# Paired output stores, a second queue for the last tiles, other quads, and a list scheduler with measured lengths

**Chip, cores, metric.** One core of one Trainium2 chip. The metric is the device time of one execution in microseconds (us); lower is better.

**Terms.** In this kernel TensorE does the matrix products, VectorE, ScalarE and GpSimd the element-wise work, and SyncE issues transfers. The profile calls them PE, DVE, ACT, POOL and SP; PEld is TensorE's weight loads, and a q (SPq, ACTq) marks the queue from which an engine issues transfers. SBUF is the on-chip memory in which the kernel's buffers lie. A transfer *lands* when its completion is signalled.

## The reference

A small speech model, two convolutions with stride 2, a projection, and a joint network. What matters here is the end: for every batch entry, time step and label step a tanh of a sum, times a 512 x 512 matrix, 16,000 rows of output.

```python
h = gelu(conv5(x, w1))[:, ::2, :]            # B=2, T=4000, D=512
f = gelu(conv5(h, w2))[:, ::2, :]            # 1000 rows for each batch entry
fe = f @ w_f                                  # (2, 1000, 512)
ge = g @ w_g                                  # (2, 8, 512)
j = tanh(fe[:, :, None, :] + ge[:, None, :, :])
return j @ w_o                                # (2, 1000, 8, 512), bfloat16
```

## The kernel before

The program is not written in the order in which it runs. Each operation is put into a plan with the buffers it reads and writes and an assumed length; a list scheduler simulates the engines with these lengths, orders each engine's queue, repeats this for 16 rounds with adjusted urgencies, and keeps the round that ends first. So an assumed length costs nothing by itself, but decides the order.

```python
def simulate(self, pred, succ, late):
    ...
        i = min(now) if e in ("pe", "sp") else min(now, key=lambda i: (late[i], i))
        ...
        start[i] = t
        free[e] = t + o.cost          # the assumed length; 0.05 us for a store on SyncE
```

The output is 125 tiles of 128 rows x 512 columns. 57 are plain: four matmuls of 512 columns, a copy to SBUF by VectorE or ScalarE, one store of 128 KB. The other 68 are made in 17 *quads* of four tiles by a seven-product scheme (28 matmuls of 256 columns) that needs sums of the inputs, made by VectorE or, for the 11 late quads, by GpSimd, and several adds on VectorE afterwards. Which quads these are is the list `WQ`; `LEAD` and `TRAIL` say how many plain tiles come before the first late quad and after the last.

```python
WQ = (5,6,10,11,12,13,16,17,18,20,21,22,24,25,26,28,29)
LEAD, TRAIL = 6,2
...
def three():                       # of a quad: tiles 0 and 1 are complete here
    ...
    tt("dve", half(1, 1), v2(y), k15, add)
    tt("dve", half(0, 1), v2(z), u2, add)
    banks.append(z)
    for t in range(2):
        send(c0 + t * P, s1 + s0 + t)          # one store for each tile, on SyncE
...
def joint_tile(jt):                # a plain tile; the last one goes in two halves
    ...
        if h == 1 or (jt % 3 == 2 if early else plain[0] % 3 == 2) and not last:
            act(o, v, ACT.Copy)
        else:
            pl.op("dve", ...tensor_copy..., vec_cost(o, (v,)))
        send(c0, s, cl, ("sp", "act")[h])
```

Of the kernel before, what the change touches and what calls it, by code (L numbers as in the profile page):

```python
# [7 lines left out]
ACT = mybir.ActivationFunctionType  # L8
ALU = mybir.AluOpType
BF16 = mybir.dt.bfloat16  # L10
FP32 = mybir.dt.float32
FP16 = mybir.dt.float16
P = 128
# [297 lines left out]
def bass_standalone__seq2seq_rnn_t_joint__speech_kernel(  # L311
# [21 lines left out]
    U = g.shape[1]  # L333
    NK = D // P
    assert (B, T, D, K, U) == (2, 4000, 512, 5, 8)
    T1, T2 = T // 2, T // 4
# [2 lines left out]
    XW = 528  # L339
    HOFF, HWID = 2, 338  # L340
    RING, LRING = 2048, 4096
    WQ = (5,6,10,11,12,13,16,17,18,20,21,22,24,25,26,28,29)
    LEAD, TRAIL = 6,2
    FROM, LATE = 64 * P, 30
    NSLOT = 12
    BU = B * U
    NT = 512
# [3 lines left out]
    with ExitStack() as es:  # L351
# [56 lines left out]

        def vec_cost(o, ins, fast=True):
            bf = fast and all(not v.psum and v.ap.dtype != FP32 for v in (o,) + tuple(ins))  # L410
            return o.ap.free_size() * (0.52e-3 if bf else 1.04e-3) + 0.065

        def memset(v):
            pl.op("pool", lambda e: e.memset(v.ap, 0.0), (), (v,))  # L414
# [5 lines left out]
        def act(o, i, func, scale=1.0, bias=None, cost=None):  # L420
            rd = (i,) if bias is None else (i, bias)
            pl.op("act", lambda e: e.activation(o.ap, i.ap, func, scale=scale,  # L422
                                                bias=0.0 if bias is None else bias.ap), rd, (o,),
                  cost or o.ap.free_size() * 0.84e-3 + (0.05 if i.psum else 0.17 if i.ap.dtype == FP32 else 0.09))

        def mm(o, pairs, start, stop, check=True):

# [557 lines left out]
        def fe(b):  # L985
            for i, m in ((1, 0), (0, 0), (1, 1), (0, 1), (2, 0), (2, 1), (1, 2), (0, 2), (2, 2), (1, 3), (0, 3), (2, 3)):
                v = ps.cols(bank(), START[i + 1] - START[i])
                sl = slice(START[i], START[i + 1])
                mm(v, [(wf_sb[k, m * P:(m + 1) * P], fT[b][k, sl]) for k in range(NK)], True, True)
                o = feT[b][m, i::3]  # L990
                if i == 1:
                    act(o, v, ACT.Copy, cost=0.54)
                else:
                    pl.op("dve", lambda e, o=o, v=v: e.tensor_copy(out=o.ap, in_=v.ap), (v,), (o,), 0.47)  # L994

        def tanh(v, k, lo=0, hi=T2):

# [44 lines left out]
        def send(c0, slot_, cl=slice(0, 512), eng="sp"):  # L1042

            lo = c0
            while lo < c0 + P:
                vv = lo // T2
                b, u, q = vv // U, vv % U, lo % T2
                n = min((vv + 1) * T2, c0 + P) - lo
                rows = (lo - c0, lo - c0 + n)
                src = oste.rows(*rows, slot_, cl) if slot_ < 4 else (  # L1050
                    ostq.rows(*rows, slot_ - 4, cl) if slot_ < 16 else ostm[slot_ - 16].rows(*rows, cl))
                dst = out[1 - b, q:q + n, u, cl]
                pl.dma(eng, lambda e, src=src, dst=dst: e.dma_start(dst, src.ap), (src,), (), slot_sem[slot_], 2 * n * P * 4)
                lo += n

        def joint_tile(jt):
            c0 = jt * P
            done.add(jt)
            ahead(c0 + P, 900)
            late = c0 >= FROM  # L1060
            r0 = c0 % (LRING if late else RING)
            j = lambda k: jL[k, r0:r0 + P] if late else jT[k][r0:r0 + P]
            early = jt < LATE
            s = jt % 4 + (16 if jt >= 20 else 0) if early else (0, 12, 1, 13, 2, 14, 3, 15)[plain[0] % 8]
            plain[0] += not early
            last = jt == ntile - 1
            for h in range(2 if last else 1):
                w = NT // 2 if last else NT
                cl = slice(h * w, (h + 1) * w)
                v = ps.cols(bank(), w)  # L1070
                mm(v, [(j(k), wo_sb[k, cl]) for k in range(NK)], True, True)
                o = oste[s, cl] if s < 4 else ostq[s - 4, cl] if s < 16 else ostm[s - 16][cl]
                if h == 1 or (jt % 3 == 2 if early else plain[0] % 3 == 2) and not last:
                    act(o, v, ACT.Copy)
                else:
                    pl.op("dve", lambda e, o=o, v=v: e.tensor_copy(out=o.ap, in_=v.ap), (v,), (o,), vec_cost(o, (v,)))  # L1076
                send(c0, s, cl, ("sp", "act")[h])

        def weights_o(wT):
            B_ = [[wo_sb[2 * i:2 * i + 2, 256 * j:256 * j + 256] for j in range(2)] for i in range(2)]  # L1080
# [6 lines left out]
        def quad_steps(q, eng, u=[0]):  # L1087

            c0 = 4 * q * P
            late = c0 >= FROM  # L1090
            soon = jt_w1 > 4 * q
            r0 = c0 % (LRING if late else RING)
            S_, kk = (sAm, kqm) if soon else (sA[u[0] % 3], kq[u[0] % (3 if late else 2)])
            k1, u2, k15 = (kk[i] for i in range(3))
            o_, s1 = (oste, 0) if soon else (ostq, 4)
            s0 = 0 if soon else 4 * (u[0] % 2)
            T_ = wTm if q < 13 else wT
            u[0] += not soon

            def A(i, j, k=None):  # L1100
                lo = r0 + 2 * i * P
                if late:
                    return jL[2 * j:2 * j + 2, lo:lo + 2 * P] if k is None else jL[2 * j + k, lo:lo + 2 * P]
                return jT[2 * j + k][lo:lo + 2 * P]

            v2 = lambda b: ps.cols(b * NT, NT).map(lambda a: a.rearrange("p (t c) -> p t c", t=2))

            def product(a, b, bk, start):
                for t in range(2):
                    sl = slice(t * P, (t + 1) * P)  # L1110
                    mm(ps.cols(bk * NT + 256 * t, 256), [(a(k, sl), b(k)) for k in range(2)], start and t == 0, True, False)

            def Ab(i, j):
                lo = r0 + 2 * i * P
                if late:
                    return lambda k, sl: jL[2 * j + k, lo + sl.start:lo + sl.stop]
                return lambda k, sl: jT[2 * j + k][lo + sl.start:lo + sl.stop]

            Sb = lambda i: lambda k, sl: S_[i, k, sl]
            Bb = lambda i, j: lambda k: wo_sb[2 * i + k, 256 * j:256 * j + 256]  # L1120
            Tb = lambda i: lambda k: T_[i, k]
            half = lambda i, j: o_[s0 + 2 * i:s0 + 2 * i + 2, 256 * j:256 * j + 256]
            held = []

            def sums():
                ahead(c0 + 4 * P, 900 if late else 300)
                for k in (None,) if late else range(2):
                    w = 2 if late else 1
                    cost = (0.58 if eng == "pool" else 0.133) * w + (0 if eng == "pool" else 0.065)
                    S1 = lambda i: S_[i] if late else S_[i, k]  # L1130
                    for o, a, b, op in ((0, A(1, 0, k), A(1, 1, k), add), (2, A(0, 0, k), A(1, 0, k), sub), (1, S1(0), A(0, 0, k), sub),
                                        (3, A(0, 1, k), S1(1), sub)):
                        v = S1(o)
                        pl.op(eng, lambda e, v=v, a=a, b=b, op=op: e.tensor_tensor(out=v.ap, in0=a.ap, in1=b.ap, op=op), (a, b), (v,), cost)  # L1134

            def one():
                held.extend(banks.pop(0) for _ in range(3))
                x, y, z = held
                product(Ab(0, 0), Bb(0, 0), x, True)
                product(Sb(1), Tb(1), y, True)  # L1140
                act(k1, v2(x), ACT.Copy)
                tt("dve", u2, v2(y), k1, add)

            def two():
                x, y, z = held
                product(Sb(0), Tb(0), z, True)
                product(Ab(0, 1), Bb(1, 0), x, False)
                tt("dve", k15, v2(z), k1, add)
                act(half(0, 0), v2(x), ACT.Copy)
                banks.append(x)  # L1150

            def three():
                x, y, z = held
                product(Sb(2), Tb(2), y, False)
                product(Sb(3), Bb(1, 1), z, False)
                tt("dve", half(1, 1), v2(y), k15, add)
                tt("dve", half(0, 1), v2(z), u2, add)
                banks.append(z)
                for t in range(2):
                    send(c0 + t * P, s1 + s0 + t)  # L1160

            def four():
                x, y, z = held
                product(Ab(1, 1), Tb(3), y, False)
                done.update(range(4 * q, 4 * q + 4))
                tt("dve", half(1, 0), v2(y), k1, add)
                banks.append(y)
                for t in range(2, 4):
                    send(c0 + t * P, s1 + s0 + t)

            return [sums, one, two, three, four]

# [130 lines left out]
```

## Time and profile before

| | before |
|---|---|
| device time, median of 3 | 262.35 us (262.25 to 262.76) |
| span of the profiled execution | 261.2 us (its time 262.84, a slow one among its fellows) |
| TensorE busy | 97%, last matmul ends at 256.73 us |
| last copy to SBUF starts (ScalarE) | 256.75 us |
| last store starts (SyncE) | 258.65 us |

The span is what the profile shows, from the first to the last instruction; the time is always longer, by 1.6 us in this kernel. Three stretches: the *front*, up to a group of eight matmuls just behind a stop near 23 us; the *stretch* from that group to the start of the last copy, in which TensorE is the bound; and the *tail*, from the last copy to the end of the span.

### The profile page before, as it was taken

How to read it: one execution, taken by the hardware profiler on the slowest of the kernel's cores; microseconds unless marked ns; L12 is line 12 of the kernel's file. 1: busy time of each engine (PE TensorE's matmuls, PEld its weight loads, DVE VectorE, ACT ScalarE, POOL GpSimd, SP SyncE). 2: the span in 40 equal slices, each digit the busy share in tenths (PEclk: the TensorE clock that was granted, in tenths of full speed). 3: DMA queues.
4: the chain of work that ended last, by engine and by line, in shares of the span. 5: the costliest groups of instructions: out<-in, count | busy, mean ns of one | idle time of the engine just before them, and what ended most of it. 6: DMA issues, size and time to landing. Idle time of an engine off the chain costs nothing.

```text
span 261.2 us, 4927 instructions
## 1 busy us (share of the span) xinstructions
PE 253.3 (97%) x1771; PEld 171.9 (66%) x1786; DVE 227.0 (87%) x447; ACT 189.2 (72%) x316; POOL 56.0 (21%) x64
## 2 busy tenths in 40 slices
PE   8999999999999899999999999999999999999992
PEld 3997764446666556566677744777777677777771
DVE  0999999999999999998557999999957778897883
ACT  2688879984365999667765569748449999999520
POOL 1000004300000000000000000000003999989930
PEclk9999999999999999999999999999999999999998
DMA  7999998979995022111112031405020364535555
GB/s 243 330 157 235 281 229 179 168 143 176 229 179 108 3 80 80 63 40 61 43 40 75 26 105 40 143 0 162 29 73 5 118 199 145 184 123 184 167 174 183
DMA packets 56710, 33.96 MB, mean 130 GB/s; under 512 B 31582, under 2 KB 56430, under 8 KB 56686
## 3 DMA queue, kind: packets, MB, share of 16 engines
q1 hardware_dynamic: 54430, 31.49, 45.7%
q0 software_dynamic: 2112, 2.10, 4.6%
q8 instruction: 14, 0.23, 0.4%
q14 instruction: 10, 0.08, 0.1%
q10 hardware_dynamic: 144, 0.07, 0.1%
HBM read 7.86 MB, written 16.38 MB: 93 GB/s over the span
## 4 chain that ended last, share of the span: by engine, by line
PE 94%; DVE 2%; ACT 1%; issue 1%; ACTq 0%
PE acc L430 93%; PE acc L523 1%; ACT jT L422 1%; DVE feT L994 1%; DVE zx L417 0%; DVE row L747 0%; ACT feT L422 0%; ACT fT L422 0%; ACT oste L422 0%; ACT sd L422 0%; DVE zero L437 0%; ACTq L272 0%
## 5 line engine op out<-in xcount | busy, mean ns | idle before, releaser
L430 PE MATMUL acc<-wo_sb,jT 128*128 128x512 bf16 (+1 forms) x199 | 44.4, 354 | 1.3 <-ACT jT L422 0.8
L1134 POOL TENSOR_TENSOR sA<-jL 128x512 f16<-128x512 bf16 x22 | 25.3, 1162 | 89.5 <-DVE feT L994 86.3
L422 ACT ACTIVATE jT<-feT,geT 128x1000 bf16<-128x1000 f32 (+9 forms) x56 | 40.7, 777 | 4.2 <-PE acc L430 2.1
L422 ACT ACTIVATE jL<-feT,geT 128x1000 bf16<-128x1000 f32 (+3 forms) x36 | 34.9, 1031 | 0.6 <-DVE feT L994 0.6
L417 DVE TENSOR_TENSOR ostq<-acc,kq 128x512 bf16<-128x512 f32 x45 | 29.8, 688 | 2.6 <-PE acc L430 2.6
L430 PEld LDWEIGHTS acc<-wo_sb,jT 128*128 128x128 bf16 x208 | 20.2, 98 | 17.0 <-ACT jT L422 1.0
L430 PE MATMUL acc<-wo_sb,jL 128*128 128x256 bf16 (+1 forms) x154 | 28.1, 313 | 0.3
L417 DVE TENSOR_TENSOR kq<-acc,kq 128x512 f32<-128x512 f32 x30 | 20.2, 689 | 6.3 <-ACT kq L422 5.2
L422 ACT ACTIVATE hT<-acc 128x334 bf16<-128x334 f32 (+3 forms) x33 | 15.2, 468 | 11.6 <-PE acc L430 11.4
L430 PE MATMUL acc<-xt,w_sb 128*128 128x252 bf16 (+1 forms) x144 | 23.5, 305 | 0.0
L1076 DVE CAST oste<-acc 128x512 bf16<-128x512 f32 (+1 forms) x27 | 18.3, 684 | 4.5 <-PE acc L430 4.3
L430 PE MATMUL acc<-row,w_sb 128*128 128x334 bf16 (+1 forms) x112 | 20.5, 306 | 0.0
L430 PE MATMUL acc<-wT,sA 128*128 128x256 f16 x144 | 20.0, 273 | 0.0
L430 PEld LDWEIGHTS acc<-wo_sb,jL 128*128 128x128 bf16 x160 | 15.6, 98 | 6.3
L430 PEld LDWEIGHTS acc<-xt,w_sb 128*128 128x128 bf16 x144 | 14.0, 98 | 7.0 <-DVE xt L417 0.3
L422 ACT ACTIVATE sd<-acc 128x334 f32<-128x334 f32 (+1 forms) x32 | 13.8, 441 | 6.1 <-PE acc L430 6.0
L430 PE MATMUL acc<-zx,w_sb 128*128 128x334 bf16 (+1 forms) x96 | 17.6, 305 | 0.0
L422 ACT ACTIVATE ostq<-acc 128x512 bf16<-128x512 f32 x21 | 12.5, 601 | 5.5 <-PE acc L430 5.4
L430 PEld LDWEIGHTS acc<-wT,sA 128*128 128x128 f16 x144 | 14.1, 98 | 3.6
L430 PE MATMUL acc<-row,w_t 128*128 128x334 bf16 (+1 forms) x80 | 14.6, 306 | 0.0
L414 POOL MEMSET zx<- 128x8 bf16 (+1 forms) x3 | 0.5, 151 | 66.1 <-PE acc L430 36.9
L430 PE MATMUL acc<-xs,w_t 128*128 128x252 bf16 (+1 forms) x76 | 14.1, 314 | 0.5 <-issue 0.5
(130 smaller groups left out, 539.6 us busy)
## 6 DMA issues: line engine op xcount, KB each, us to landing
out_dram<-ostq SPq DMA_DIRECT2D x67, 128.0 KB, 2.0
w_sb<-in_w_dram SPq DMA_DIRECT2D x10, 512.0 KB, 6.3
out_dram<-oste SPq DMA_DIRECT2D x40, 128.0 KB, 1.9
xr<-in_x_dram SPq DMA_DIRECT2D x2, 512.0 KB, 4.0
half<-w_sb POOLq DMA_DIRECT2D x2, 512.0 KB, 6.5
half<-w_t POOLq DMA_DIRECT2D x2, 512.0 KB, 5.2
wf_sb<-in_w_f_dram SPq DMA_DIRECT2D x1, 512.0 KB, 6.8
wg_sb<-in_w_g_dram SPq DMA_DIRECT2D x1, 512.0 KB, 5.6
```

The costliest lines, as they stand in the source:

```text
L414: pl.op("pool", lambda e: e.memset(v.ap, 0.0), (), (v,))
L417: pl.op(eng, lambda e: e.tensor_tensor(out=o.ap, in0=a.ap, in1=b.ap, op=op), (a, b), (o,), vec_cost(o, (a, b)))
L422: pl.op("act", lambda e: e.activation(o.ap, i.ap, func, scale=scale, bias=0.0 if bias is None else bias.ap), rd, (o,), cost or o.ap.free_s ...
L430: ins = e.matmul(o.ap, lhsT=l.ap, rhs=r.ap, start=start and n == 0, stop=stop and n == len(pairs) - 1, skip_group_check=not check)
L523: ins = e.transpose(pv.ap[:, r, k, :], xr[rt].h[:, 2 * r + pp, k, :], ident.h[:, :])
L994: pl.op("dve", lambda e, o=o, v=v: e.tensor_copy(out=o.ap, in_=v.ap), (v,), (o,), 0.47)
L1076: pl.op("dve", lambda e, o=o, v=v: e.tensor_copy(out=o.ap, in_=v.ap), (v,), (o,), vec_cost(o, (v,)))
L1134: pl.op(eng, lambda e, v=v, a=a, b=b, op=op: e.tensor_tensor(out=v.ap, in0=a.ap, in1=b.ap, op=op), (a, b), (v,), cost)
```

## The change

Its intent: fewer and earlier stores, and orders that fit the engines' real speed. Cut to its core:

```diff
-    WQ = (5,6,10,11,12,13,16,17,18,20,21,22,24,25,26,28,29)
-    LEAD, TRAIL = 6,2
+    WQ = (5,6,10,11,12,13,16,17,18,20,21,22,23,24,26,27,28)
+    LEAD, TRAIL = 4,4
 ...                                  # assumed lengths, us
-            return o.ap.free_size() * (0.52e-3 if bf else 1.04e-3) + 0.065
+            return o.ap.free_size() * (0.52e-3 if bf else 1.04e-3) + 0.07
-                  cost or ... (0.05 if i.psum else 0.17 if i.ap.dtype == FP32 else 0.09))
+                  cost or ... (0.05 if i.psum else 0.09 if bias is None else 0.18))
-                    act(o, v, ACT.Copy, cost=0.54)
+                    act(o, v, ACT.Copy, cost=0.45)
-                    pl.op("dve", ...tensor_copy..., 0.47)
+                    pl.op("dve", ...tensor_copy..., 0.475)
 ...                                  # stores
-                pl.dma(eng, ..., slot_sem[slot_], 2 * n * P * 4)
+                pl.dma(eng, ..., slot_sem[slot_], 2 * n * P * 4).cost = 0.48
+        def send2(c0, s1, s0):
+            if c0 // T2 != (c0 + 2 * P - 1) // T2:      # the pair crosses a sequence
+                for t in range(2):
+                    send(c0 + t * P, s1 + s0 + t)
+                return
+            ...
+            dst = out[1 - vv // U, q:q + 2 * P, vv % U, :].rearrange("(t p) c -> p t c", t=2)
+            pl.dma("sp", ..., slot_sem[s1 + s0], 2 * P * NT * 2).cost = 0.48
 ...                                  # plain tiles
-                if h == 1 or (jt % 3 == 2 if early else plain[0] % 3 == 2) and not last:
+                end = jt > ntile - 6
+                by_act = h == 1 if last else jt % 2 == 0 if end else jt % 3 == 2 if early else plain[0] % 3 == 2
+                if by_act:
-                send(c0, s, cl, ("sp", "act")[h])
+                send(c0, s, cl, "act" if end and by_act else "sp")
 ...                                  # quads, steps three and four
-                for t in range(2):
-                    send(c0 + t * P, s1 + s0 + t)
+                send2(c0, s1, s0)
```

More of the change, by code (lines that the diff above doesn't have):

```diff
@@ L423, in act @@
                                                 bias=0.0 if bias is None else bias.ap), rd, (o,),
-                  cost or o.ap.free_size() * 0.84e-3 + (0.05 if i.psum else 0.17 if i.ap.dtype == FP32 else 0.09))
+                  cost or o.ap.free_size() * 0.84e-3 + (0.05 if i.psum else 0.09 if bias is None else 0.18))
         def mm(o, pairs, start, stop, check=True):
@@ L991, in fe @@
                 if i == 1:
-                    act(o, v, ACT.Copy, cost=0.54)
+                    act(o, v, ACT.Copy, cost=0.45)
                 else:
-                    pl.op("dve", lambda e, o=o, v=v: e.tensor_copy(out=o.ap, in_=v.ap), (v,), (o,), 0.47)
+                    pl.op("dve", lambda e, o=o, v=v: e.tensor_copy(out=o.ap, in_=v.ap), (v,), (o,), 0.475)
         def tanh(v, k, lo=0, hi=T2):
@@ L1052, in send @@
                 dst = out[1 - b, q:q + n, u, cl]
-                pl.dma(eng, lambda e, src=src, dst=dst: e.dma_start(dst, src.ap), (src,), (), slot_sem[slot_], 2 * n * P * 4)
+                pl.dma(eng, lambda e, src=src, dst=dst: e.dma_start(dst, src.ap), (src,), (), slot_sem[slot_], 2 * n * P * 4).cost = 0.48
                 lo += n
+        def send2(c0, s1, s0):
[3 more added lines that the diff above has]
+                return
+            vv, q = c0 // T2, c0 % T2
+            src = (oste if s1 == 0 else ostq)[s0:s0 + 2]
+            dst = out[1 - vv // U, q:q + 2 * P, vv % U, :].rearrange("(t p) c -> p t c", t=2)
+            pl.dma("sp", lambda e: e.dma_start(dst, src.ap), (src,), (), slot_sem[s1 + s0], 2 * P * NT * 2).cost = 0.48
         def joint_tile(jt):
@@ L1167, in four @@
                 banks.append(y)
-                for t in range(2, 4):
-                    send(c0 + t * P, s1 + s0 + t)
+                send2(c0 + 2 * P, s1, s0 + 2)
             return [sums, one, two, three, four]
```

## The prediction

> **What bounds the kernel now.** I read the page first (busy shares, slices, the chain that ended last), then the waits of TensorE and of the SyncE queue, then the last 17 us in order of time, then the same for the two places where TensorE stops.
>
> ```profile
> PE 253.3 (97%) x1771; PEld 171.9 (66%) x1786; DVE 227.0 (87%) x447; ACT 189.2 (72%) x316; POOL 56.0 (21%) x64
> ...
> PE   8999999999999899999999999999999999999992
> ...
> PE acc L430 93%; PE acc L523 1%; ACT jT L422 1%; DVE feT L994 1%; DVE zx L417 0%; DVE row L747 0%; ACT feT L422 0%; ACT fT L422 0%; ACT oste L422 0%; ACT sd L422 0%; DVE zero L437 0%; ACTq L272 0%
> ```
>
> TensorE is busy 97% of 261.2 us, and the chain lies on it for 94%. So the first question for any change here is whether it takes work off TensorE. To see how full "busy" is, I counted the columns in the source: 1,728 matmuls (convolutions, the projection, 57 single tiles of 4 x 512 columns, 17 quads of 28 x 256) make 578,370 columns; at 2.4 GHz plus 2.5 ns each that is 241.0 + 4.3 = 245.3 us. The warm-up (4.3 us) and the transposes (2.5 us) add 6.8, the start 1.2: 253.3. TensorE's last matmul ends at 256.73 by the timeline. So at most some 3.4 us (less the roughly 0.3 us by which the last matmul's own length exceeds its pace, so about 3) of stalls lie inside, of which the page shows little:
>
> ```profile
> 78.66 0.55 PE L430 MATMUL acc<-gT,wg_sb 128*128 128x16 bf16 x16
> 79.36 7.00 PE L430 MATMUL acc<-fT,wf_sb 128*128 128x333 bf16 x48 [0.16 <-ACT fT L422]
> ...
> 89.47 1.68 PE L430 MATMUL acc<-wo_sb,jT 128*128 128x512 bf16 x7 [0.84 <-ACT jT L422]
> ```
>
> The third column on is the work; the bracket is idle time before it and who ended it. The real stop is before 89.47: the first output tile waits for the first tanh rows, 0.84 us. Another 0.5 us stands near 23.4. Between 165 and 256.7 us TensorE waited for nothing by the waits view; it is busy 91.3 of 91.7 us, and part of the 0.4 is missing records (a group of four 512-wide matmuls shows as three, with a hole of 0.05).
>
> Then the end:
>
> ```profile
> 252.47 5.12 SPq L1053 DMA_DIRECT2D out_dram<-ostq  x10
> ...
> 256.75 0.38 ACT L422 ACTIVATE oste<-acc 128x256 bf16<-128x256 f32 x1 [3.31 <-PE acc L430]
> 257.17 0.38 ACTq L1053 DMA_DIRECT2D out_dram<-oste  x1
> 257.64 0.46 SPq L1053 DMA_DIRECT2D out_dram<-oste  x1
> 258.14 0.46 SPq L1053 DMA_DIRECT2D out_dram<-ostq  x1
> 258.65 0.46 SPq L1053 DMA_DIRECT2D out_dram<-oste  x1
> ```
>
> The last result is in SBUF at 257.13, but SyncE starts its last store at 258.65. It issues 13 stores in a row from 252.47, one per 0.51 us (5.12 / 10), without catching up: the queue is about 1.7 us behind (the half tile that VectorE finished at 256.90 could have gone at 256.95). This store's landing is 1.8 us after its start (260.45), and the span ends at 261.24, so 0.8 us of closing follow. The end is set by SyncE's queue, not by TensorE or bandwidth: the DMA engines move nothing in the last 1.2 us.
>
> **What the Trainium skill says.** "DMA: Bandwidth & Descriptors", section "Issuing engines are not separate DMA queues": transfers from all engines share the same 16 DMA engines; several issuing engines save only the sequencer's time to start them. That is the resource short here; the trace agrees, with 0.33 to 0.46 us per issue and a lag of 1.7 us. The same page, section "Anatomy of one DMA", puts the constant part at about 2.0 us, mostly the receipt of the last write; the trace has 2.0 us median from issue to landing for 128 KB, and 2.1 for the one store from ScalarE's queue. So landing itself cannot be shortened, only started sooner. "TensorE: Matmul & The Clock Gate", section "Wait — 56ns, not 53.3ns?", gives N/2.4 GHz + 2.5 ns per warm matmul, used above; the trace agrees: 20 matmuls of 512 columns near 202 us take 4.48 us, less one length of 0.379, over 19 = 0.216 us each.
>
> **The change part by part.**
> 1. *Paired stores.* A quad sends four tiles of 128 KB as four transfers, plus one more for each tile that crosses a 1000-row sequence. Now two tiles go in one of 256 KB, unless the pair crosses such an edge. Counting the edges: 141 transfers before; 34 pairs, of which 7 cross, so 27 transfers fewer: 114. SyncE saves about 27 x 0.48 = 13 us of issue time over the span, none of it on the path except in the last 12 us. Readiness does not move: in step "three" the two tiles of a pair were already sent together. Landing of a pair takes longer (estimated 0.3 to 0.6 us at the last slices' 170 to 330 GB/s), in transfers for whose buffers nobody waits: no VectorE or ScalarE wait for an output transfer is listed.
> 2. *ScalarE's queue for the last tiles.* Of tiles 120 to 124, the even ones are now copied by ScalarE and stored from its own queue. It costs ScalarE about 0.38 us each, where it was idle 3.31 us before the last copy. A plain tile takes TensorE 4 x 0.216 = 0.86 us, so SyncE gets one store per 1.7 us and issues one in 0.46: the lag is gone. The last start becomes the half tile on ScalarE: 0.44 us after TensorE's end, at 257.17 on the old clock. Landing 2.0 to 2.1 gives 259.2 to 259.3, against 260.45: **1.2 us gained**. If landing is quicker in the emptier queues, 1.4.
> 3. *Other quads.* Still 17 in all, 11 of them late, so the matmul count and the 245.3 us stay. But 4 single tiles instead of 6 come before the first late quad, and 4 instead of 2 after the last. GpSimd makes the quads' sums, 44 of 1.16 us, one per 1.11 us, from 198.36 to 250.75, nearly without a stop. Slack before: the first late quad's sum is ready at 204.95 and used at 206.96, so 2.0 us; the last is ready at 250.75 and used at 253.08, so 2.3 us. Two tiles less at either end are 1.73 us: slack 0.3 and 0.6 us remain. So no stall expected, but very little room; **0 to +0.3 us**.
> 4. *Scheduler's lengths.* They issue nothing themselves; they reorder VectorE and ScalarE. The new ones fit: 0.602 for a 512-wide fp32 VectorE operation, the trace's two in 1.28 with 0.69 for one, so 0.60 apart; the scattered feT copy 0.45 on ScalarE, the trace 0.46 between starts at 198.22 and 198.68, where the old number was 0.54. A store now takes 0.48 of its queue instead of 0.05, against 0.51 measured. A better order can at most remove the stop at 89 us (0.84 plus what the matmul's pipeline hides) and crumbs; there, bf16 transforms sit between the feT copies on VectorE, which is a matter of order. I expect **0.4 us gained**, with as much uncertainty in either direction.
>
> Sum: 1.2 + 0.4 - 0.1 (a little stalling from 3) = 1.5 us; with 0.15 for the chance of quicker landings 1.65. So 262.35 - 1.65 = 260.7 us.
>
> **Rivals.** *A: the tail is the whole gain.* If the order changes nothing net, 262.35 - 1.2 = 261.1. For it: TensorE lists hardly any waits, so order can hardly help. *B: the tight sums stall TensorE.* Slack of 0.3 us at the first late quad may turn into a wait for GpSimd, or tanh work is put late by the new order (ScalarE is full from 200 to 240 us); each could cost 0.5 to 1.5 us, eating the tail: 261.5 to 262.5. Against it: the scheduler knows GpSimd's length (1.16 modelled, 1.11 measured) and can move a single tile up. *C: reordering clears most stops.* TensorE ends 1.5 us sooner and the tail gives 1.3: 259.5. For it: the old model was wrong about queue time, so its choice among 16 rounds was of a wrong end. *D: the saved issue time is hidden anyway*, because the landing of a 256 KB pair takes the place of the backlog: 262. Against it: single tiles, not pairs, are last, and four single tiles (3.5 us) follow the last pair.
>
> **Range and chances.** The tail's 1.2 is the solid part; order and stalls move it by about 1 us each way. That gives 259.5 to 261.9 for 8 in 10. 2% is 5.2 us; TensorE's 245.3 us of columns are untouched, and about 3 us of stalls plus 1.5 of tail is all there is, so faster by over 2% is nearly impossible. Slower by as much would need a new stall that the list scheduler did not see.
>
> **What would show it.** The SyncE queue should have 27 issues fewer, and no run of issues behind one another at the end; the last store start within 0.5 us of TensorE's last matmul, and the span's end 2.9 to 3.3 us after it instead of 4.5. TensorE's last matmul at 255.5 to 257.0. The stop before the first tanh-fed tile should be under 0.84 us. GpSimd should stay without gaps, and the waits of TensorE for its sums under 0.5 us. I am wrong if a wait of matmuls or weight loads for sA or jL appears between 200 and 255 us, if TensorE's end moves by more than 1.2 us, or if the end still hangs on SyncE's queue.

## The result

The changed kernel takes 260.58 us (260.34 to 261.16, 4 runs) against 262.39 us (262.25 to 262.76, 4 runs), ratio 0.9932, 95% interval 0.9913 to 0.9951. A ratio here is the mean time of one kernel's fast runs over that of the other's in the same rounds, so not quite the ratio of the medians. In a later set of rounds the same two kernels gave 0.9918 (0.9896 to 0.994).

The page after: the span, the busy times (us, share, instructions), and the pairs among the transfers (count, size, us to landing).

```profile
span 258.6 us, 4891 instructions
...
PE 252.5 (98%) x1772; PEld 171.4 (66%) x1786; DVE 227.1 (88%) x446; ACT 189.7 (73%) x317; POOL 56.0 (22%) x64
...
out_dram<-ostq SPq DMA_DIRECT2D x24, 256.0 KB, 2.3
...
out_dram<-oste SPq DMA_DIRECT2D x3, 256.0 KB, 2.1
```

TensorE's busy time is the same but for 0.8 us; 27 transfers are pairs, as counted. The instructions are 36 fewer. So the work has not changed, and the gain must lie in waits. They are in two places.

**The stop before the first tanh-fed tile.** The timeline near 85 us, first of the kernel before, then of the changed one: start, length, engine, source line, operation, tiles (`feT` holds the projected rows, `jT` the tanh of the sums).

```profile
85.28 1.56 DVE L994 COPY feT<-acc 128x333 f32<-128x333 f32 x3
86.69 0.85 DVE L598 SCALAR_TENSOR_TENSOR row<-r 128x668 bf16<-128x668 f32 x1
87.44 1.08 DVE L994 COPY feT<-acc 128x334 f32<-128x334 f32 x2
```

```profile
85.04 2.49 DVE L994 COPY feT<-acc 128x333 f32<-128x333 f32 x5
87.38 0.87 DVE L598 SCALAR_TENSOR_TENSOR row<-r 128x668 bf16<-128x668 f32 x1
...
88.48 2.54 PE L430 MATMUL acc<-wo_sb,jT 128*128 128x512 bf16 x11
```

Before, VectorE puts a transform for the next convolution (`row<-r`, 0.85 us) between two groups of the copies that feed tanh; the last copies end at 88.52, the last tanh of the first tile follows, and TensorE waits. In the changed order the five copies come first and end at 87.53; the line of the first tanh-fed matmuls has no wait behind it any more. From the group near 23 us to that line it was 65.55 us (23.92 to 89.47), and is now 64.80 us (23.68 to 88.48): 0.75 us gained.

**The tail.** The last entries of the timeline after, to be held against those in the prediction:

```profile
252.18 3.63 PE L430 MATMUL acc<-wo_sb,jL 128*128 128x512 bf16 x20
252.66 0.98 SPq L1065 DMA_DIRECT2D out_dram<-ostq  x2
...
253.96 2.07 SPq L1053 DMA_DIRECT2D out_dram<-ostq  x2
...
255.84 0.38 ACT L422 ACTIVATE oste<-acc 128x256 bf16<-128x256 f32 x1 [1.14 <-PE acc L430]
256.08 0.43 SPq L1053 DMA_DIRECT2D out_dram<-oste  x1
256.26 0.34 ACTq L1053 DMA_DIRECT2D out_dram<-oste  x1
```

SyncE's last store now starts 0.24 us after the last copy starts; before it was 1.90 us (258.65 - 256.75). The last store of all starts on ScalarE's queue 0.42 us after it, as soon as its data are there. The tail falls from 4.50 us (261.25 - 256.75) to 2.79 us (258.63 - 255.84).

The sum of the span: front 0.24 us earlier (23.92 to 23.68), the stop 0.75, the rest of the stretch 0.08 lost (167.28 to 167.36), the tail 1.71: 2.62 us, which is 261.25 - 258.63. The front's share is chance, as the repeats below show. And the time gained is 1.8 us, not 2.6: part of that is the slower than usual execution that the profile of before had caught (262.84 us), part is met again below.

### The profile page after: what moved, and what is told of

It reads as the page before. It is cut to its first block, busy times and chain, and to the rows that moved or that the text cites. A ratio compares the mean times of both kernels' runs of the same rounds, so it can differ in the third digit from the quotient of the medians.

```text
span 258.6 us, 4891 instructions
## 1 busy us (share of the span) xinstructions
PE 252.5 (98%) x1772; PEld 171.4 (66%) x1786; DVE 227.1 (88%) x446; ACT 189.7 (73%) x317; POOL 56.0 (22%) x64
## 4 chain that ended last, share of the span: by engine, by line
PE 88%; DMA 5%; SPq 3%; DVE 1%; issue 1%; ACT 0%; DVEq 0%
PE acc L430 88%; SPq L461 3%; DMA w_sb<-in_w_dram 2%; DMA xs<-in_x_dram 1%; DMA xr<-in_x_dram 1%; DMA out_dram<-ostq 1%; DVE kq L417 0%; DVE ty L598 0%; DVE xt L417 0%; DVE ostq L417 0%; DVE w_t L598 0%; ACT fT L422 0%; ACT cs L422 0%; ACT oste L422 0%; SPq L448 0%
## 5 line engine op out<-in xcount | busy, mean ns | idle before, releaser
L430 PE MATMUL acc<-wo_sb,jT 128*128 128x512 bf16 (+1 forms) x199 | 45.0, 353 | 0.5
L422 ACT ACTIVATE jL<-feT,geT 128x1000 bf16<-128x1000 f32 (+3 forms) x36 | 35.8, 1054 | 0.6 <-DVE feT L994 0.6
L430 PE MATMUL acc<-wo_sb,jL 128*128 128x256 bf16 (+1 forms) x155 | 28.9, 313 | 0.3
L417 DVE TENSOR_TENSOR kq<-acc,kq 128x512 f32<-128x512 f32 x30 | 19.6, 683 | 3.9 <-PE acc L430 2.6
L1089 DVE CAST oste<-acc 128x512 bf16<-128x512 f32 (+1 forms) x25 | 16.9, 684 | 4.6 <-PE acc L430 4.5
```

The source lines that it names most:

```text
L417: pl.op(eng, lambda e: e.tensor_tensor(out=o.ap, in0=a.ap, in1=b.ap, op=op), (a, b), (o,), vec_cost(o, (a, b)))
L422: pl.op("act", lambda e: e.activation(o.ap, i.ap, func, scale=scale, bias=0.0 if bias is None else bias.ap), rd, (o,), cost or o.ap.free_s ...
L430: ins = e.matmul(o.ap, lhsT=l.ap, rhs=r.ap, start=start and n == 0, stop=stop and n == len(pairs) - 1, skip_group_check=not check)
L1089: pl.op("dve", lambda e, o=o, v=v: e.tensor_copy(out=o.ap, in_=v.ap), (v,), (o,), vec_cost(o, (v,)))
```

## The experiments

Twelve runs were made, three of them repeats (b_again, a_again, a_oldq). All gave correct results. The parts that touch stores alone are clean: in the traces of b_pairs, a_nopair and a_noactq the four compute engines do the same operations in the same order as in the kernel that was edited, and in b_endq only VectorE and ScalarE differ, in the last tiles. Lengths and quads change the order itself. In the table, *stretch* is from the eight-matmul group near 23 us to the start of the last copy, *tail* from there to the end of the span (both from one profile each); the ratio is to the kernel before of the same rounds.

| kernel | stretch | tail | ratio (95%) |
|---|---|---|---|
| before | 232.83 | 4.50 | |
| b_again: before, repeated | 232.88 | 4.37 | 1.0002 (0.998 to 1.0025) |
| b_pairs: before + pairs | 232.84 | 3.21 | 0.9977 (0.996 to 0.9993) |
| b_endq: before + last tiles on ScalarE's queue | 232.84 | 3.45 | 0.997 (0.9954 to 0.9986) |
| b_stores: before + both | 232.85 | 3.13 | 0.9964 (0.9941 to 0.9988) |
| b_len: before + lengths | 232.17 | 3.91 | 0.9958 (0.994 to 0.9976) |
| b_wq: before + quads, LEAD, TRAIL | 233.09 | 4.04 | 1.0018 (0.9997 to 1.0038) |
| after | 232.16 | 2.79 | 0.9932 (0.9913 to 0.9951) |
| a_again: after, repeated | 232.20 | 2.80 | 0.9918 (0.9896 to 0.994) |
| a_nopair: after without pairs | 232.65 | 3.12 | 0.995 (0.9935 to 0.9966) |
| a_noactq: after without ScalarE's queue | 232.18 | 2.79 | 0.9942 (0.9924 to 0.9959) |
| a_nolen: after with old lengths | 233.34 | 2.79 | 0.999 (0.9974 to 1.0007) |
| a_nowq: after with old quads | 232.18 | 3.06 | 0.9937 (0.9922 to 0.9952) |
| a_oldq: the same, repeated | 232.19 | 3.08 | 0.9936 (0.9913 to 0.9958) |

The stretch repeats within 0.05 us for the same order, so 0.2 us in it can be read from one profile; the times scatter by 1 to 1.6 us from run to run. Between repeats the scatter is in the front: the eight-matmul group starts at 23.92 and 23.46 us in the two profiles of before, at 23.68 and 24.29 in the two of after. One part of the change has no run of its own, the 0.48 us that the scheduler now counts for a store. a_nowq has it and b_len has not, and otherwise the two differ only in the stores and in who copies the last tiles: TensorE's order is the same and the stretch too (232.18 and 232.17). So with the old quads it does nothing there; with the new ones it is untested.

### b_pairs: the pairs alone

```diff
-                for t in range(2):
-                    send(c0 + t * P, s1 + s0 + t)
+                send2(c0, s1, s0)
```
(and the same in step four; the scheduler still counts 0.05 us for any store). The four compute engines' orders are those of before to the last instruction.

> Kernel before with the paired stores alone; by the built program the order on TensorE, VectorE, ScalarE and GpSimd is exactly that of before, only SyncE issues 27 transfers fewer. Theory (the end hangs on SyncE's lag of 1.7 us): three of the 13 stores in a row at the end fall away, 3 x 0.51 = 1.5 us, so TensorE's end stays at 256.7, the tail from there shrinks from 4.5 to 3.0 to 3.3 us, time 261.1 to 261.4. Rival (issue time is hidden, or the landing of 256 KB takes its place): tail stays above 4 us, time 262.1 or more.

Measured: 261.49 us against 262.12, ratio 0.9977. The end of its timeline:

```profile
255.57 0.40 SPq L1065 DMA_DIRECT2D out_dram<-ostq  x1
256.02 0.47 SPq L1053 DMA_DIRECT2D out_dram<-oste  x1
256.43 0.38 ACT L422 ACTIVATE oste<-acc 128x256 bf16<-128x256 f32 x1 [3.31 <-PE acc L430]
256.53 0.45 SPq L1053 DMA_DIRECT2D out_dram<-ostq  x1
256.85 0.37 ACTq L1053 DMA_DIRECT2D out_dram<-oste  x1
257.02 0.45 SPq L1053 DMA_DIRECT2D out_dram<-oste  x1
```

SyncE's last start is 0.59 us behind the last copy instead of 1.90, and the tail is 3.21 us. The theory's tail (3.0 to 3.3) holds; the time is just above its range. The rival of a hidden issue time falls, for the span. In device time the pairs alone gain 0.6 us (means 262.09 and 261.50), half of what the tail shows: the mean span is 1.16 us shorter (260.49 to 259.33), but 0.56 us more lies outside it (told under a_again).

### b_endq: ScalarE's queue alone

```diff
-                if h == 1 or (jt % 3 == 2 if early else plain[0] % 3 == 2) and not last:
+                end = jt > ntile - 6
+                by_act = h == 1 if last else jt % 2 == 0 if end else ...
-                send(c0, s, cl, ("sp", "act")[h])
+                send(c0, s, cl, "act" if end and by_act else "sp")
```

> Kernel before with the last single tiles split between VectorE and ScalarE and ScalarE's stores on its own queue; TensorE's order is that of before. Theory: SyncE loses two of its last 13 stores, 2 x 0.51 = 1.0 us, the tail shrinks from 4.5 to about 3.5 us, time 261.4. Rival: the transfers share the engines anyway and the time stays at 262.3.

Measured: 261.39 us, ratio 0.997, tail 3.45: as expected. SyncE's last store starts 0.63 us behind the last copy.

### b_stores: both

```diff
+                send2(c0, s1, s0)              # as in b_pairs
+                send(c0, s, cl, "act" if end and by_act else "sp")     # as in b_endq
```

> Kernel before with both store changes (pairs, and ScalarE's queue for the last tiles), old lengths, old quads. Each alone gave 0.9977 and 0.9970. If both shorten the same lag of SyncE's queue, they do not add: 0.9960 to 0.9970, tail 2.8 to 3.1 us. If they are separate gains: 0.9947. With the lengths (0.9958) and the quads (1.0018) the first would make the whole 0.994, as measured.

Measured: 0.9964, tail 3.13 us. The interval of the time covers both expectations. The profiles decide: against the mean tail of before (4.43) the parts gain 1.22 and 0.98 us, both together 1.30, not 2.20. They shorten the same lag, and either does most of it.

### a_noactq and a_nopair: each taken out of the changed kernel

```diff
-                send(c0, s, cl, "act" if end and by_act else "sp")
+                send(c0, s, cl, ("sp", "act")[h])
```

> Changed kernel with the stores of the last single tiles on SyncE again (who copies them stays). The last half tile stays on ScalarE's queue as before. If pairs and the four single tiles clear the lag: within 0.3 us of the changed kernel. If ScalarE's queue is what carries the 1.2 us, as the prediction had it: 261.5 to 261.8. I lean to the first, 260.8.

Measured: 260.30 us against 261.76, 0.9942, tail 2.79 us, SyncE's last store 0.22 us behind the last copy. The prediction gave the whole 1.2 us to ScalarE's queue. Its stores of tiles 120 and 122 can go without a loss that shows once pairs and four plain tiles at the end are there. (The last half tile is stored from ScalarE's queue in every kernel here.)

```diff
-                send2(c0, s1, s0)
+                for t in range(2):
+                    send(c0 + t * P, s1 + s0 + t)
```

> Changed kernel with single stores again; every engine but SyncE issues exactly what the changed kernel does. If pairs are needed for the end: SyncE is late again and the tail grows by 0.5 to 1.5 us, 261.1 to 262.1. If the last stores on ScalarE's queue and the four last single tiles already clear the lag: within 0.3 us of the changed kernel, 260.5 to 260.9, with the tail at 2.8 to 3.0 us. I lean to a small loss, 260.9.

Measured: 260.52 us, 0.995, close to the changed kernel. But the profile shows something new, in its timeline:

```profile
249.84 6.30 SPq L1053 DMA_DIRECT2D out_dram<-ostq  x12
...
251.10 2.09 DVE L417 TENSOR_TENSOR ostq<-acc,kq 128x512 bf16<-128x512 f32 x3 [0.43 <-DMA out_dram<-ostq]
...
251.85 0.61 PE L430 MATMUL acc<-wT,jL 128*128 128x256 f16 x4 [0.28 <-DVE ostq L417]
```

Twelve single stores stand in SyncE's queue; VectorE waits 0.43 us for one of them to free its output buffer, and TensorE 0.28 us for VectorE. The stretch is 0.45 to 0.49 us longer than the changed kernel's. With the new quads a late queue no longer delays only the end; it holds buffers, and through them TensorE. Pairs remove that.

### b_len and a_nolen: the lengths alone, and the change without them

```diff
-            return o.ap.free_size() * (0.52e-3 if bf else 1.04e-3) + 0.065
+            return o.ap.free_size() * (0.52e-3 if bf else 1.04e-3) + 0.07
```
(with the three other lengths of the change; no store, quad or issue time).

> Kernel before with the scheduler's new operation lengths alone (no store changed, no issue time). By the built program ScalarE's and VectorE's order up to the late stage is that of the changed kernel. Theory: the order gives TensorE's gain, 0.25 us before 27 us and 0.74 us in the stop before the first tanh-fed tile; that tile starts at 88.5 instead of 89.5, TensorE ends at 255.7 to 255.9, tail still 4.5 us, time 261.3 to 261.5. Rival: the 0.9 us came from the late stage's other quads, or differs from run to run: first tile at 89.4, time 262.2 or more.

Measured: 260.92 us against 262.12, 0.9958. The stretch is 0.67 us shorter, at the stop before the first tanh-fed tile, as in the changed kernel. The front was earlier still than said (22.92 us), but the seven profiles with the new lengths have it at 22.92 to 24.29 us and the seven with the old ones at 23.31 to 23.93: the 0.25 us that I had put down to the lengths is not shown to be theirs. The tail came out 0.5 us shorter than before's although no store was touched, which no one expected: SyncE's last run of single stores begins 5.05 us before the last copy (250.04 to 255.09), in before 4.28 us (252.47 to 256.75). Its last store starts 1.26 us behind the last copy (256.35 - 255.09) instead of 1.90. The new order lets SyncE begin that run sooner.

> Changed kernel with the old operation lengths; stores, quads and issue time as changed. Theory: the first tanh-fed tile at 89.4 again, TensorE's end about 0.9 us later, tail unchanged at 2.8: 261.4 to 261.6. Rival (the lengths do nothing): 260.6.

Measured: 261.65 us against 261.76, 0.999 (0.9974 to 1.0007). Without the lengths nearly nothing is left of the gain, though the tail is still 2.79 us: the stretch is 233.34, 1.16 us longer than the changed kernel's mean (232.18). 0.75 of it is the stop, back with the wait of before; the other 0.4 is a loss that the new quads have with the old lengths, seen next. The four lengths were only changed together; which of them does it is not tested.

### b_wq, a_nowq, a_oldq: the quads

```diff
-    WQ = (5,6,10,11,12,13,16,17,18,20,21,22,24,25,26,28,29)
-    LEAD, TRAIL = 6,2
+    WQ = (5,6,10,11,12,13,16,17,18,20,21,22,23,24,26,27,28)
+    LEAD, TRAIL = 4,4
```

> Kernel before with the new list of quads and LEAD, TRAIL 4, 4 alone. Theory of the prediction: no gain and 0 to 0.3 us lost to tight sums, 262.3 to 262.7. Rival: four single tiles at the end (0.86 us of TensorE each, 0.5 us of SyncE) let SyncE's queue catch up by about 2 x 0.36 us, so the tail is some 0.7 us shorter, 261.7.

Measured: 262.50 us against 262.12, 1.0018. The stretch is 0.25 us longer. From its timeline:

```profile
239.97 2.25 ACT L422 ACTIVATE jL<-feT,geT 128x1000 bf16<-128x1000 f32 x2
242.01 0.69 ACT L422 ACTIVATE ostq<-acc 128x512 bf16<-128x512 f32 x1
242.13 1.04 PE L430 MATMUL acc<-wT,sA 128*128 128x256 f16 x8
242.48 0.70 ACT L422 ACTIVATE kq<-acc 128x512 f32<-128x512 f32 x1
...
243.24 0.11 PEld L430 LDWEIGHTS acc<-wo_sb,jL 128*128 128x128 bf16 x2 [0.35 <-ACT kq L422]
...
250.64 0.60 ACT L422 ACTIVATE ostq<-acc 128x512 bf16<-128x512 f32 x1 [2.68 <-DMA out_dram<-ostq]
```

A weight load waits 0.35 us for ScalarE's copy `kq`, which comes late, behind two tanh operations and another copy. Start to start, this is TensorE's only stop after 93 us that before has not (both lose 0.1 us near 162): from 242.13 eight matmuls of 0.109 us would end at 243.00, the next starts at 243.24, 0.24 us late, and that is the whole loss. ScalarE also stands 2.7 us before a copy whose output buffer is still being stored, but that comes seven microseconds later and TensorE loses nothing to it; the first profile of the changed kernel has the same wait (2.5 us), the second has not, and their stretches agree (232.16 and 232.20).

In a_nolen the stop for `kq` is there again (0.26 us at 243.42), and a second one of 0.22 us at 252.78, where VectorE had waited 0.3 us for an output buffer. In the changed kernel a plain tile stands at the place of the first stop (matmuls from 242.83), and there is none. The waits for the sums from GpSimd, which the prediction feared, are in no list. The tail is shorter than before's, as the rival said, but by 0.4 us instead of 0.7. With 0.25 us more stretch and 0.19 us more outside the span (told under a_again) that comes to about nothing, and the 0.18% measured is at the edge of its interval: alone, the quads gain nothing and may lose a little.

> Changed kernel with the old list of quads and LEAD, TRAIL 6, 2. If the quads are neutral, as the prediction had it: 260.3 to 260.6 (it has no tight sums, so it may even be the best). If the four single tiles at the end are part of the shorter tail: 260.8 to 261.3.

Measured: 260.23 us against 261.76, 0.9937.

> The changed kernel with the old quads once more, now in the same rounds as the changed kernel. The new quads alone cost 0.18%, so if that holds here this is faster by 0.1 to 0.2% than the changed kernel (ratio 0.9915 to 0.992). If the new lengths have taken that cost away, both are the same within 0.1%.

Measured: 260.74 us against the changed kernel's 260.38 in the same rounds (0.9936 and 0.9918, intervals overlapping). With the new lengths the quads' cost in the stretch is gone (232.18 and 232.19 against 232.16 and 232.20), so my expectation of 0.1 to 0.2% faster was wrong. What they give is 0.3 us of tail: with the old quads the last store starts just as early, but lands 2.1 us after its start instead of 1.8, which is all of it. The windows view of the microsecond from 256 to 257, in which the last stores are under way, for the old quads (a_oldq) and then the changed kernel; the two last numbers are the DMA engines' share (1.04 is to be read as full) and GB/s:

```profile
256.00:257.00 1.00, 0.00 (x0) 0.00 (x0) 0.00 (x0) 0.00 (x0) 0.00 (x0) 1.00 1.04 356
```

```profile
256.00:257.00 1.00, 0.00 (x0) 0.00 (x0) 0.00 (x0) 0.23 (x1) 0.00 (x0) 1.00 0.41 133
```

These last stores start at 255.95 and 256.26; in the microsecond from its own start each has a share of 1.04 and 0.61. With only two plain tiles after the last quad the DMA engines are still full when the last store is issued, with four they are not. In device time these 0.3 us are within the noise (intervals above).

### b_again, a_again: both kernels once more

```diff
(no difference)
```

> The kernel before once more, unchanged: a null test of the rounds and a second profile. Ratio 1.000 within 0.15%. If the first profile is typical, first tanh-fed tile some 65.5 us after the matmul group near 23 us, and a tail of 4.5 us after the start of the last copy; but the kernels with the old stores and other changes had tails of 3.9 and 4.0 us, so 3.9 to 4.5 is what I expect.

Measured: ratio 1.0002, tail 4.37, as expected. The first profile of before was thus typical in its stretch and tail.

> The changed kernel once more: ratio to the kernel before 0.993 within 0.15%, stretch to the first tanh-fed tile 64.8 us, tail 2.8 us.

Measured: ratio 0.9918, stretch and tail as expected. The mean spans of these rounds are 260.98 us (6 runs of before) and 258.63 us (6 of after): 2.35 us, against 0.68 + 1.57 = 2.25 from the stretches and tails of the two profiles. The mean times are 262.57 and 260.50: 2.07 us. The missing 0.28 us lies outside the span: the time exceeds the span by 1.59 us in before and by 1.87 us in after, within 0.02 us in every set of rounds in which they ran. Other kernels have other offsets (b_len 1.60, b_wq 1.78, a_nowq 1.80, b_pairs 2.17), most of them steady from run to run; those of b_stores and a_nolen move between 1.73 and 2.11. What it consists of no view shows, and I leave it open.

No kernel tried is clearly faster than the changed one. So a gain in the span is not all gained in time, and a tail that one profile shows must be checked against the times.

## Why the prediction was right, and where its steps were not

- **Time.** 260.7 predicted, 260.58 measured, inside 259.5 to 261.9. "Within 2%" was right. TensorE's columns are the floor, and its 245.3 us are untouched. That the number came within 0.2 us is partly luck: the gain foretold, 1.65 us in all, was 2.25 us in the span; 0.28 us of this is lost outside the span, which the prediction did not know of, and the two sets of rounds differ too (means 1.8 and 2.1 us faster).
- **The tail as bound by SyncE's queue: right in mechanism.** b_pairs and b_endq, which leave TensorE's order alone, shorten the tail by 1.2 and 1.0 us. "The last store start within 0.5 us of TensorE's last matmul" came true, and the end lies 2.8 us after it, a little below the 2.9 to 3.3 that I gave.
- **Its size: 1.2 us predicted, 1.6 us measured in the span** (4.37 to 2.80, the repeats). The term mis-sized is the landing of the last store: taken as 2.0 to 2.1 us ("cannot be shortened"), it was 1.8, which the prediction had as a chance only; the closing after it was about 0.6 us (258.63 - 256.26 - 1.8) instead of 0.8. The short landing goes with DMA engines that are not full (0.61 in the microsecond from its start, against 1.04 in a_oldq, where it took 2.1); no run tests that alone. In time 0.28 us of the gain is given back outside the span.
- **Who does it: wrong in part.** The prediction gave the 1.2 us to ScalarE's queue, and to the pairs nothing on the path "except in the last 12 us". Either alone does most of it in the tail, and in the changed kernel ScalarE's queue can be dropped for all but the last half tile without a loss that shows (a_noactq).
- **The order: 0.4 us predicted, 0.67 us in the stretch.** The place was right, the wait before the first tanh-fed tile, and the cause too: transforms between the feT copies. The size of the stop was misread: of the 0.84 us shown, 0.21 is a missing record. Kernels with the same order show either eight matmuls after a wait of 0.63 us or seven after 0.84 to 0.88. Start to start (87.89 to 89.47 before, 87.64 to 88.48 after), less 0.57 us for four matmuls of that kind and 0.21 for the missing record, the stop was 0.80 us and 0.06 is left: nearly the whole stop went. I had counted half. The new order also costs a little, which I had not counted: near 161 us TensorE loses 0.3 us behind a weight load that waits 0.6 us for ScalarE's `sd`, where before it loses 0.1. The lengths also help the tail by 0.5 us where the old stores are kept, which I had not seen.
- **The quads: right in total, wrong in reason.** "0 to +0.3 us" from tight sums. The first late quad's sum was indeed tight, as the timeline of the changed kernel shows: ready at 204.04 and used at 204.32, the 0.3 us foretold, without a wait. At the other end it was not: the last sum was ready at 248.86 (247.68 + 1.18) and used at 251.31, 2.4 us and not 0.6: the last quad's use of it came 1.8 us sooner than before, but the sum itself 1.9 us. The cost of the new quads lies elsewhere: with the old lengths a copy of ScalarE comes late (0.24 us in b_wq, 0.26 in a_nolen), and twice VectorE waits for an output buffer and TensorE for VectorE (0.22 us in a_nolen, 0.45 in a_nopair). In the full change there is neither. The step "for whose buffers nobody waits" failed too: with the new quads ScalarE waits 2.3 to 2.8 us for a store's landing in five of six profiles. But TensorE loses nothing to that wait; what costs it 0.45 us in a_nopair is VectorE's wait.
- **Slips in the sums,** which move nothing: at 170 to 330 GB/s another 128 KB takes 0.4 to 0.8 us, not 0.3 to 0.6 (the trace after has 0.3: 2.3 us to landing for a pair, 2.0 for one tile); and the last matmul's length exceeds its pace by 0.16 us (0.379 - 0.216), not 0.3.
- **The rivals.** A (tail alone) is refuted by b_len and a_nolen: the lengths are about half of the gain. B (a stall in the late stage) is what b_wq and a_nolen show, not by its first cause, the sums, but close to its second, ScalarE full of tanh work. C (order clears most stops) is half true: 0.7 of its 1.5 us. D (hidden anyway) is refuted by b_pairs for the span; in time half of the pairs' gain is missing there.

None of the signs that were to show me wrong came: no wait for sA or jL after 100 us, TensorE's end 0.9 us earlier (255.81), and the last start no longer on SyncE.

The two lines on which the statement about the first late quad's sum rests, GpSimd's sum and its use on TensorE in the changed kernel:

```profile
202.89 1.15 POOL L1147 TENSOR_TENSOR sA<-sA,jL 128x512 f16<-128x512 f16 x1
...
204.32 1.04 PE L430 MATMUL acc<-wT,sA 128*128 128x256 f16 x8
```

## What to carry to other kernels

When the busiest engine is full, look at what follows its last instruction: an issuing queue that ran 1.9 us behind cost 1.0 to 1.3 us of the span here (b_endq, b_pairs, b_stores), and there were several ways to empty it (fewer and larger stores, a second queue, cheap-to-store work at the end), whose gains did not add. A scheduler that is fed assumed lengths can put a transform in front of the copies that a stalled engine needs; measure start-to-start spacings and feed those. And test the parts of a combined change one by one: here one part gains nothing alone, shortens the tail beside the others, and costs 0.25 to 0.5 us of the stretch if another part is missing.

## What the Trainium skill lacked or had wrong

- "DMA: Bandwidth & Descriptors", section "Issuing engines are not separate DMA queues", says that issuing from several engines saves only the sequencer's time, "which is usually small relative to the DMA itself", and gives no number there (elsewhere it has a count in cycles for earlier chips, in a table on trn3, and none for trn2 by name). Here a store of 128 KB took SyncE 0.33 to 0.47 us and back-to-back stores came 0.51 us apart; with 13 in a row the last one started 1.8 to 1.9 us after the last copy had started, where 0.24 us is possible: over a third of a tail of 4.4 us.
- No page read says how this cost depends on the size; here it hardly does: in the changed kernel the median was 0.35 to 0.37 us for 128 KB or less and 0.38 to 0.40 us for a pair of 256 KB.
- "DMA: Bandwidth & Descriptors", section "Anatomy of one DMA — SWDGE (gpsimd) path", puts the constant part near 2.0 us, for transfers that GpSimd issues; it gives no such sum for stores that SyncE or ScalarE issue. For the last two 64 KB stores the runs show 1.7 and 1.8 us in the changed kernel, and 2.0 to 2.3 us in b_endq, b_stores and a_oldq, with the DMA engines at 0.9 or more in the microsecond from the start of the last store.
- No page read has the time outside the profile's span: 1.59 us in one kernel, 1.60 to 2.17 us in others that differ only in order or stores.
- No page read warns that a missing matmul record at the head of a group looks like a longer wait: 0.84 to 0.88 us shown with seven records, 0.63 us with eight.
